# A convolution and spectral-mixing kernel: layout of the mixed modes, order of the band's set-up, of small copies and loads, and of the last stores

## The chip, the core and the metric

The kernel runs on one NeuronCore of a Trainium2 chip. The metric is the device time of one execution in microseconds (us), median of five runs. A core has five engines with a queue of instructions each: TensorE (PE in the profile; its weight loads are listed as PEld), VectorE (DVE), ScalarE (ACT), GpSimd (POOL) and SyncE (SP), and 16 DMA engines that move what SP, ACT and POOL issue. SBUF is the on-chip memory of 128 partitions; PSUM is where TensorE writes its results, eight banks of 512 float32 per partition.

## The reference

The input x is 8 x 3264 x 192 (batch, sequence, channels), float32. First a causal convolution over the sequence with 7 taps, whose softmaxed weights are one set for each of 8 heads of 24 channels. Then 64 Fourier modes of the result are mixed by complex 192 x 192 matrices, transformed back and added, and a dense layer with a ReLU comes on top.

```python
w = softmax(weight)                                   # 8 heads x 7 taps
a[b, s, h, :] = sum_k w[h, k] * x_padded[b, s + k, h, :]
X = rfft(a, axis=1)[:, :64]
Yr = Xr @ w_r - Xi @ w_i ; Yi = Xr @ w_i + Xi @ w_r   # one 192 x 192 pair for each mode
y = irfft(Y, n=3264, axis=1)                          # the other modes are zero
u = a + y
out = u + maximum(u @ w_ch, 0)
```

## The kernel before

Line numbers are those of the kernel before. The order of the instructions on each engine is the order of the Python text: there is no scheduler. The sequence is cut into 27 windows of 122 rows (`WIN`), each held with 6 more rows (`OV`) on 128 partitions, in one bfloat16 tile `x_all[partition, batch, window, channel]`. The last window has only 92 valid rows.

*Set-up.* SP loads eight windows of batch 0 as float32 (`x32`, L103), which ACT casts into `x_all` (L172); all the other windows come through POOL's DMA queue, which casts on the way (L61; the first window of batch 0 in two small pieces, L66 and L67). The taps come through ACT's queue (`wraw`, L99). DVE builds `diagc`, a band index of 38 columns for each group of 32 partitions (L146 to L149), and `ident` (L151), then the softmax of the taps (L166 to L179). TensorE spreads the taps over the partitions (L186). For each tap DVE makes a 128 x 304 product (`scaled`, L196: 8 heads x 38 columns) and TensorE adds it up through an identity into two PSUM banks, `bps`, both with the same content (L201). ACT copies the groups 0 and 2 of partitions out of one bank (L209), DVE the groups 1 and 3 out of the other (L211), into `cband`, the convolution's band matrix of each head.

*Convolution and DFT.* For each of 24 units (a batch and 8 to 10 windows) TensorE convolves (`conv_half`, L268), ACT or DVE writes the result back over the input (L275, L277), and TensorE adds the 64 modes over the windows (`dft_unit`, L290; the table `fst` is made by `f_turns` and `f_sin`). Only rows 0 to 121 of a window are written back. For windows 6, 13 and 20, rows 122 to 127 are therefore fetched from the next window by three SBUF-to-SBUF copies on SP (L366), since these windows are stored after their successors.

*Mixing.* The 64 modes are taken four at a time in 16 groups (`mix(g)`, L463), whose weights POOL loads ahead (`load_weights`, L259). Between the groups TensorE transposes the convolved rows into `cTa` and `cTb` (`t_next`, L426), and DVE and ACT copy them out. After each second group `mix_t` transposes the mixed values (L493) and DVE copies them into `yeT` (L494). `yeT` holds, for each of two halves of the channels, the mode components as outer index and the batch as inner one, so one batch is every eighth element. `y_back` transposes part of `yeT` back into `zy` (L485); the later groups reach `zy` by an SP DMA (L475). `prefill` starts the first output banks early, and `keep_warm` is a matmul without use.

*Output.* `zw_mm` multiplies `yeT` by the dense layer's matrix (L510). Then 108 units (half of the batches, window, pair of batches) follow: TensorE adds the dense layer of the convolved rows and the inverse transform (`z_ops`, L542), ACT applies the ReLU (L564), TensorE adds the inverse transform of the modes themselves (`y_ops`, L559), DVE adds the convolved rows (L594), and after each second unit SP stores 128 rows of four batches (L604), 384 KB; the window 26 goes out as 80 and 12 rows. The windows are taken in the order `worder`, by remainder modulo 7.

```python
    worder = sorted(range(NWIN), key=lambda w: (w % CH, w // CH))
```

Of the kernel before, what the change touches and what calls it, by code (L numbers as in the profile page):

```python
# [18 lines left out]
def kernel(  # L19
# [53 lines left out]
    def load_last():  # L73
# [29 lines left out]
    nc.sync.dma_start(out=x32[:], in_=bass.AP(tensor=x.tensor, offset=x.offset + (WIN * 10 - OV) * D,  # L103
                                              ap=[[D, P], [WIN * D, 8], [1, D]]))
# [4 lines left out]
    load_win(0, 1, 9)  # L109
    sidx = sp.tile([P, NWIN], F32, tag="sidx")  # L110
# [7 lines left out]
    load_unit(1, 0)  # L118
# [7 lines left out]
    for b in range(1, B):  # L126
        for u in range(3):
            if (b, u) != (1, 0):
                load_unit(b, u)
# [13 lines left out]

    NB = 32 + OV
    diagc = sp.tile([P, NB], F32, tag="diagc")
    nc.vector.memset(diagc[0:32, 0:OV], -1.0)  # L146
    for g in range(4):
        i0 = OV if g == 0 else 0
        nc.vector.tensor_copy(out=diagc[32 * g:32 * g + 32, i0:NB],  # L149
                              in_=diag[32 * g:32 * g + 32, 32 * g - OV + i0:32 * g + 32])  # L150
    nc.vector.tensor_scalar(out=ident[:], in0=diag[:], scalar1=0.0, scalar2=None, op0=ALU.is_equal)  # L151
# [29 lines left out]

    ps1 = ExitStack()
# [12 lines left out]
    for k in range(KK):  # L195
# [4 lines left out]
        for o in bps:  # L200
            nc.tensor.matmul(o[:, 0:H * NB], ident[:], scaled[:, k, :, :].rearrange("p h i -> p (h i)"),  # L201
                             start=(k == 0), stop=(k == KK - 1))
    make_k(1)
    for g in range(4):
        i0 = OV if g == 0 else 0
        dst = cband[32 * g:32 * g + 32, :, 32 * g - OV + i0:32 * g + 32]
        srcv = bps[g % 2][32 * g:32 * g + 32, 0:H * NB].rearrange("p (h i) -> p h i", h=H)[:, :, i0:NB]
        if g % 2 == 0:
            nc.scalar.copy(out=dst, in_=srcv)  # L209
        else:  # L210
            nc.vector.tensor_copy(out=dst, in_=srcv)  # L211
# [32 lines left out]
    yeT = constp.tile([P, 2, 2 * MODES * B], BF16, tag="yeT")  # L244
# [118 lines left out]


    for w in (6, 13, 20):
        nc.sync.dma_start(out=x_all[WIN:P, :, w, :], in_=x_all[0:OV, :, w + 1, :])  # L366
# [112 lines left out]
    def y_back(half):  # L479
        tp = pt.tile([P, 1024], BF16, tag="p", name="yb")  # L480
        n = 16 * YPE
        for i in range(4):
            for e in range(2):
                c0 = D * i + 64 * e
                nc.tensor.transpose(tp[0:n, c0:c0 + P], yeT[:, e, 4 * half + i:n * B:B], ident[:])  # L485
# [3 lines left out]
    def mix_t(g, ymix):  # L489
# [4 lines left out]
        nc.vector.tensor_copy(out=yeT[:, :, P * (g // 2):P * (g // 2) + P], in_=et)  # L494
# [261 lines left out]
```

## Time and profile before

| | |
|---|---|
| median of 5 runs | 180.55 us (180.28 to 181.05) |
| the profiled execution, its own time | 180.28 us |
| its span, first to last instruction | 178.5 us |
| PE busy, PEld busy | 149.3 us (84%), 130.4 us (73%) |
| DVE, ACT, POOL busy | 127.9, 112.6, 48.8 us |
| granted TensorE clock, mean | 0.994 |
| HBM read, written | 40.28 MB, 21.01 MB |
| last weights used from | 107.11 us |
| last DVE add ends | 173.79 us |

A span runs from an execution's first to its last instruction; the time of a run is some 1.8 us more. In the views, "us busy" of an engine is the sum of its instructions' times in a stretch, the DMA share is the mean busy share of the 16 DMA engines (packets that overlap count twice, so it can exceed 1), and GB/s is what they wrote: x and the weights arrive as float32 and are written as bfloat16, so a rate of 206 GB/s there is 412 GB/s read. The chain of waits goes back from the last instruction to whatever released each step.

### The profile page before, as it was taken

What the parts mean: (1) busy time and instruction counts of PE and PEld (TensorE: products, weight loads), DVE (VectorE), ACT (ScalarE), POOL (GpSimd) and SP (SyncE); (2) the same over time, 40 slices, a digit from 0 to 9 for tenths busy, and PEclk for the clock granted to TensorE, in tenths of its full rate; (3) what the DMA queues carried; (4) which work ended last, traced back from release to release, by engine and by line L of the source; (5) the groups of instructions that cost most, each with busy time, mean ns of one, the idle gap of its engine ahead of it and who ended that gap; (6) DMA issues with size and microseconds to landing.
All of it is one profiled execution on the core that took longest, in us unless ns stands there. A gap on an engine that the chain in (4) does not pass through costs nothing.

```text
span 178.5 us, 5425 instructions
## 1 busy us (share of the span) xinstructions
PE 149.3 (84%) x2132; PEld 130.4 (73%) x2132; DVE 127.9 (72%) x260; ACT 112.6 (63%) x188; POOL 48.8 (27%) x74
## 2 busy tenths in 40 slices
PE   0474779988899978887886978999999999999980
PEld 0243459878788868886775866799999999999950
DVE  5879975562553546966766425699999999999990
ACT  2356983555557635775766214588888888888850
POOL 7998342549222343541543000000000000000000
PEclk9999999999999999999999999999999999999997
DMA  4999999999999999999999980668999999999996
GB/s 132 212 190 192 192 192 192 191 190 192 192 192 195 202 206 208 204 207 207 205 208 205 208 145 11 208 222 281 373 357 327 368 339 355 346 311 368 339 327 229
DMA packets 65813, 42.04 MB, mean 236 GB/s; under 512 B 29212, under 2 KB 65788, under 8 KB 65788
## 3 DMA queue, kind: packets, MB, share of 16 engines
q0 software_dynamic: 36048, 19.75, 79.5%
q1 hardware_dynamic: 29738, 21.96, 37.1%
q8 instruction: 16, 0.26, 0.6%
q14 instruction: 9, 0.07, 0.1%
q10 hardware_dynamic: 2, 0.00, 0.0%
HBM read 40.28 MB, written 21.01 MB: 343 GB/s over the span
## 4 chain that ended last, share of the span: by engine, by line
PE 59%; DMA 17%; DVE 15%; issue 4%; POOL 1%; ACT 1%; DVEq 0%; POOLq 0%; ACTq 0%
PE z L542 19%; PE z L559 14%; DMA wt<-in_moe_w_i_dram 11%; PE xp L290 8%; PE cp L268 8%; DMA wt<-in_moe_w_r_dram 6%; DVE x_all L277 5%; PE tp L426 2%; PE bps L201 2%; PE yp L463 2%; PE tp L302 1%; DVE kprod L223 1%; PE z L524 1%; DVE xs L294 1%; DVE turns L221 1%
## 5 line engine op out<-in xcount | busy, mean ns | idle before, releaser
L594 DVE TENSOR_TENSOR t<-z,x_all 128x384 f32<-128x384 f32 x108 | 59.5, 557 | 3.3 <-PE z L559 1.7
L564 ACT ACTIVATE z<-z 128x384 f32<-128x384 f32 x108 | 50.9, 475 | 12.0 <-PE z L542 1.4
L542 PE MATMUL z<-zw,gst 64*128 64x384 bf16 x204 | 46.5, 323 | 0.0
L559 PE MATMUL z<-zy,gst 64*128 64x384 bf16 x204 | 46.2, 323 | 0.2
L542 PE MATMUL z<-win,cTa 64*128 64x192 bf16 x375 | 41.1, 243 | 0.0
L275 ACT CAST x_all<-cp 122x864 bf16<-122x864 f32 (+2 forms) x34 | 28.6, 879 | 16.5 <-PE cp L268 16.3
L542 PEld LDWEIGHTS <-cTa 64*128 64x128 bf16 x450 | 35.2, 94 | 2.7
L268 PE MATMUL cp<-x_all,cband 128*128 128x192 bf16 (+2 forms) x192 | 26.7, 293 | 7.5 <-DVE x_all L277 3.4
L268 PEld LDWEIGHTS <-cband 128*128 128x128 bf16 x192 | 20.1, 111 | 11.6 <-issue 4.2
L277 DVE CAST x_all<-cp 122x768 bf16<-122x768 f32 (+2 forms) x14 | 14.7, 1054 | 14.3 <-PE cp L268 13.9
L61 POOL DMA_DIRECT2D x_all<-in_x_dram x23 | 22.1, 974 | 8.1 <-DMA x_all<-in_x_dram 7.3
L290 PE MATMUL xp<-x_all,fst 122*128 122x192 bf16 (+1 forms) x216 | 22.3, 253 | 0.9 <-DVE x_all L277 0.5
L431 ACT COPY cTa<-tp 128x854 bf16<-128x854 bf16 (+1 forms) x16 | 14.0, 911 | 10.2 <-PE tp L426 10.1
L290 PEld LDWEIGHTS <-fst 122*128 122x128 bf16 (+1 forms) x216 | 18.6, 101 | 2.1 <-DVE x_all L277 0.7
L542 PEld LDWEIGHTS <-gst 64*128 64x128 bf16 x204 | 19.1, 94 | 0.6 <-issue 0.6
L542 PE MATMUL z<-win,cTb 64*128 64x192 bf16 x135 | 19.2, 243 | 0.0
L542 PE MATMUL z<-wB,cTa 64*128 64x192 bf16 x75 | 18.2, 243 | 0.0
L559 PEld LDWEIGHTS <-gst 64*128 64x128 bf16 x204 | 16.2, 93 | 1.0 <-POOLq L576 0.9
L542 PEld LDWEIGHTS <-cTb 64*128 64x128 bf16 x162 | 14.4, 94 | 1.1
L430 DVE COPY cTa<-tp 128x854 bf16<-128x854 bf16 (+1 forms) x17 | 10.6, 622 | 5.4 <-PE tp L426 5.0
L259 POOL DMA_DIRECT2D wt<-in_moe_w_r_dram x14 | 8.6, 612 | 19.9 <-PE tp L426 6.4
L426 PE MATMUL tp<-ident,x_all 122*128 122x122 bf16 x216 | 13.6, 217 | 0.0
(105 smaller groups left out, 172.0 us busy)
## 6 DMA issues: line engine op xcount, KB each, us to landing
out_dram<-t SPq DMA_DIRECT2D x52, 384.0 KB, 4.1
wt<-in_moe_w_r_dram POOLq DMA_DIRECT2D x14, 288.0 KB, 11.0
wt<-in_moe_w_i_dram POOLq DMA_DIRECT2D x14, 288.0 KB, 11.2
x_all<-in_x_dram POOLq DMA_DIRECT2D x8, 432.0 KB, 12.2
x_all<-in_x_dram POOLq DMA_DIRECT2D x7, 480.0 KB, 11.9
x_all<-in_x_dram POOLq DMA_DIRECT2D x8, 384.0 KB, 13.9
x<-in_x_dram SPq DMA_DIRECT2D x1, 768.0 KB, 5.0
fst<-in_moe_w_r_dram POOLq DMA_DIRECT2D x2, 288.0 KB, 10.3
```

Source lines behind the costliest of these rows:

```text
L61: nc.gpsimd.dma_start(out=x_all[:, b, c0:c0 + n, :], in_=src)
L268: nc.tensor.matmul(cp[:, j, 0:GRP * n].rearrange("p (w e) -> p w e", w=n), cband[:, h, :], x_all[:, b, w0:w0 + n, GRP * h:GRP * h + GRP], ...
L275: nc.scalar.copy(out=dst, in_=srcv)
L277: nc.vector.tensor_copy(out=dst, in_=srcv)
L290: nc.tensor.matmul(xp[:, 0:D], fst[0:k, c, :], x_all[0:k, b, c, :], start=(u == FIRST[b] and c == w0), stop=(u == LAST[b] and c == w0 + n ...
L426: nc.tensor.transpose(tp[:, WIN * k:WIN * k + WIN], slot_lhsT(p, k0 + k), ident[0:WIN, 0:WIN])
L430: nc.vector.tensor_copy(out=got[0][0], in_=got[0][1])
L431: nc.scalar.copy(out=got[1][0], in_=got[1][1])
L542: return nc.tensor.matmul(o, lhsT, rhs, start=start, stop=stop, skip_group_check=True, tile_position=(lo, 0))
L559: return [lambda: nc.tensor.matmul(zp[:, 0:2 * D], gst[lo:hi, WIN * w:WIN * w + P], zwi[(h, 1, k)][lo:hi, :], start=False, stop=(r == 1), ...
L564: return nc.scalar.activation(out=zp[:, 0:2 * D], in_=zp[:, 0:2 * D], func=ACT.Relu)
L594: add = nc.vector.tensor_tensor(out=t[:, 2 * k:2 * k + 2, :], in0=zp[:, 0:2 * D].rearrange("p (i e) -> p i e", i=2), in1=x_all[:, 4 * h + ...
```

## The change

Six things change, and nothing of what is computed. (1) The float32 load of eight windows becomes two loads of four, on SP and on ACT. (2) `diagc` and `ident` are made behind the softmax, and each `bps` bank holds four heads instead of all eight; ACT copies out the bank of the first four heads for all four groups of partitions, DVE the other. (3) The loads of batch 1's first two units are moved, the first ahead of the two small pieces of batch 0's first window. (4) `yeT` has the batch outside and the mode components inside, so one batch is contiguous; the copy of L494 now reads every eighth element. (5) Window 26 comes last in `worder`, and the three copies of L366 stand after the loop over the groups. (6) `y_back` stands after `mix_t`, and five matmuls without use follow in each of the groups 11, 12 and 13, into the bank (`junk`) that the third `prefill` takes later.

```diff
--- before.py
+++ after.py
@@ -100,13 +100,16 @@
                         in_=bass.AP(tensor=weight.tensor, offset=weight.offset, ap=[[H * KK, 1], [1, H * KK]]))
 
     x32 = sp.tile([P, 8, D], F32, tag="x32")
-    nc.sync.dma_start(out=x32[:], in_=bass.AP(tensor=x.tensor, offset=x.offset + (WIN * 10 - OV) * D,
-                                              ap=[[D, P], [WIN * D, 8], [1, D]]))
+    for q, eng in enumerate((nc.sync, nc.scalar)):
+        eng.dma_start(out=x32[:, 4 * q:4 * q + 4, :],
+                      in_=bass.AP(tensor=x.tensor, offset=x.offset + (WIN * (10 + 4 * q) - OV) * D,
+                                  ap=[[D, P], [WIN * D, 4], [1, D]]))
     load_unit(0, 2)
     diag = sp.tile([P, P], F32, tag="diag")
     nc.gpsimd.iota(diag[:], pattern=[[-1, P]], base=0, channel_multiplier=1,
                    allow_small_or_imprecise_dtypes=True)
     load_win(0, 1, 9)
+    load_unit(1, 0)
     sidx = sp.tile([P, NWIN], F32, tag="sidx")
     nc.gpsimd.iota(sidx[:], pattern=[[WIN, NWIN]], base=0, channel_multiplier=1,
                    allow_small_or_imprecise_dtypes=True)
@@ -115,7 +118,7 @@
     nc.gpsimd.iota(midx[:], pattern=[[1, MODES // 2], [MODES // 2, 2]], base=0, channel_multiplier=0,
                    allow_small_or_imprecise_dtypes=True)
     load_unit(0, 0)
-    load_unit(1, 0)
+    load_unit(1, 1)
     diag2 = sp.tile([P, MODES], F32, tag="diag2")
     nc.gpsimd.iota(diag2[:], pattern=[[-2, 2], [-4, MODES // 2]], base=0, channel_multiplier=1,
                    allow_small_or_imprecise_dtypes=True)
@@ -125,7 +128,7 @@
     wB0 = constp.tile([P, D], BF16, tag="wB0")
     for b in range(1, B):
         for u in range(3):
-            if (b, u) != (1, 0):
+            if (b, u) not in ((1, 0), (1, 1)):
                 load_unit(b, u)
         if b == 3:
             nc.gpsimd.memset(xt[:, :, 1, :, :], 0.0)
@@ -140,15 +143,6 @@
     ones = sp.tile([1, P], BF16, tag="ones")
     nc.vector.memset(ones[:], 1.0)
     nc.vector.memset(cband[:], 0.0)
-
-    NB = 32 + OV
-    diagc = sp.tile([P, NB], F32, tag="diagc")
-    nc.vector.memset(diagc[0:32, 0:OV], -1.0)
-    for g in range(4):
-        i0 = OV if g == 0 else 0
-        nc.vector.tensor_copy(out=diagc[32 * g:32 * g + 32, i0:NB],
-                              in_=diag[32 * g:32 * g + 32, 32 * g - OV + i0:32 * g + 32])
-    nc.vector.tensor_scalar(out=ident[:], in0=diag[:], scalar1=0.0, scalar2=None, op0=ALU.is_equal)
 
     halfpi = sp.tile([P, 1], F32, tag="halfpi")
     nc.vector.memset(halfpi[:], math.pi / 2)
@@ -179,6 +173,15 @@
     nc.vector.tensor_tensor(out=wrow[:], in0=wexp[:],
                             in1=wrec[:, :].unsqueeze(2).to_broadcast([1, H, KK]), op=ALU.mult)
 
+
+    NB = 32 + OV
+    diagc = sp.tile([P, NB], F32, tag="diagc")
+    nc.vector.memset(diagc[0:32, 0:OV], -1.0)
+    for g in range(4):
+        i0 = OV if g == 0 else 0
+        nc.vector.tensor_copy(out=diagc[32 * g:32 * g + 32, i0:NB],
+                              in_=diag[32 * g:32 * g + 32, 32 * g - OV + i0:32 * g + 32])
+    nc.vector.tensor_scalar(out=ident[:], in0=diag[:], scalar1=0.0, scalar2=None, op0=ALU.is_equal)
     ps1 = ExitStack()
     pconv = ps1.enter_context(tc.tile_pool(name="pconv", bufs=3, space=PSUM))
     pxx = ps1.enter_context(tc.tile_pool(name="pxx", bufs=1, space=PSUM))
@@ -197,18 +200,20 @@
                                        in0=diagc[:, :].unsqueeze(1).to_broadcast([P, H, NB]), scalar=float(k),
                                        in1=wsb[:, :, k:k + 1].to_broadcast([P, H, NB]),
                                        op0=ALU.is_equal, op1=ALU.mult)
-        for o in bps:
-            nc.tensor.matmul(o[:, 0:H * NB], ident[:], scaled[:, k, :, :].rearrange("p h i -> p (h i)"),
+        for half, o in enumerate(bps):
+            nc.tensor.matmul(o[:, 0:H // 2 * NB], ident[:],
+                             scaled[:, k, 4 * half:4 * half + 4, :].rearrange("p h i -> p (h i)"),
                              start=(k == 0), stop=(k == KK - 1))
     make_k(1)
     for g in range(4):
         i0 = OV if g == 0 else 0
-        dst = cband[32 * g:32 * g + 32, :, 32 * g - OV + i0:32 * g + 32]
-        srcv = bps[g % 2][32 * g:32 * g + 32, 0:H * NB].rearrange("p (h i) -> p h i", h=H)[:, :, i0:NB]
-        if g % 2 == 0:
-            nc.scalar.copy(out=dst, in_=srcv)
-        else:
-            nc.vector.tensor_copy(out=dst, in_=srcv)
+        for half, o in enumerate(bps):
+            dst = cband[32 * g:32 * g + 32, 4 * half:4 * half + 4, 32 * g - OV + i0:32 * g + 32]
+            srcv = o[32 * g:32 * g + 32, 0:H // 2 * NB].rearrange("p (h i) -> p h i", h=H // 2)[:, :, i0:NB]
+            if half == 0:
+                nc.scalar.copy(out=dst, in_=srcv)
+            else:
+                nc.vector.tensor_copy(out=dst, in_=srcv)
 
 
     WFAC = -TWOPI * (1.0 - 4e-7) / S
@@ -241,7 +246,7 @@
 
     gst = constp.tile([P, GW], BF16, tag="gst")
 
-    yeT = constp.tile([P, 2, 2 * MODES * B], BF16, tag="yeT")
+    yeT = constp.tile([P, 2, B, 2 * MODES], BF16, tag="yeT")
 
 
 
@@ -360,10 +365,6 @@
 
     ps1.close()
     conv_stack.close()
-
-
-    for w in (6, 13, 20):
-        nc.sync.dma_start(out=x_all[WIN:P, :, w, :], in_=x_all[0:OV, :, w + 1, :])
     workp = early_stack.enter_context(tc.tile_pool(name="work", bufs=3, side="right"))
     tailp = early_stack.enter_context(tc.tile_pool(name="tails", bufs=2, side="right"))
     pza = ctx.enter_context(tc.tile_pool(name="pza", bufs=3, space=PSUM))
@@ -482,7 +483,7 @@
         for i in range(4):
             for e in range(2):
                 c0 = D * i + 64 * e
-                nc.tensor.transpose(tp[0:n, c0:c0 + P], yeT[:, e, 4 * half + i:n * B:B], ident[:])
+                nc.tensor.transpose(tp[0:n, c0:c0 + P], yeT[:, e, 4 * half + i, 0:n], ident[:])
         nc.vector.tensor_copy(out=zy[0:n, 4 * half:4 * half + 4, :],
                               in_=tp[0:n, 0:4 * D].rearrange("p (b e) -> p b e", b=4))
 
@@ -491,7 +492,9 @@
         et = zt[:, 256:512].bitcast(BF16)[:, 0:2 * P].rearrange("p (t k) -> p t k", t=2)
         for t in range(2):
             nc.tensor.transpose(et[:, t, :], ymix[:, 64 * t:64 * t + P], ident[:])
-        nc.vector.tensor_copy(out=yeT[:, :, P * (g // 2):P * (g // 2) + P], in_=et)
+        q = 16 * (g // 2)
+        nc.vector.tensor_copy(out=yeT[:, :, :, q:q + 16],
+                              in_=et.rearrange("p t (q b) -> p t b q", b=B))
 
 
 
@@ -507,7 +510,7 @@
             zp = banks[i % len(banks)]
             o = zp[:, D * i:D * i + D] if len(banks) == 1 else zp[:, 0:D]
             for e, wn in ((0, win0), (1, win1)):
-                nc.tensor.matmul(o, yeT[:, e, b:2 * MODES * B:B], wn[:, :],
+                nc.tensor.matmul(o, yeT[:, e, b, :], wn[:, :],
                                  start=(e == 0), stop=(e == 1), skip_group_check=True)
         zt = zwip.tile([P, 2 * D], BF16, tag=f"zw{h}{k}", name="zw")
         if len(banks) == 2:
@@ -605,7 +608,7 @@
 
 
     CH = 7
-    worder = sorted(range(NWIN), key=lambda w: (w % CH, w // CH))
+    worder = sorted(range(NWIN), key=lambda w: (w == NWIN - 1, w % CH, w // CH))
     wq = [(0, worder[0]), (0, worder[1])]
     for i in range(2, NWIN):
         wq.append((0, worder[i]))
@@ -626,13 +629,13 @@
         return py.tile([P, 512], F32, tag="y", name="z")
 
     def prefill():
-        zps.append(bank(len(zps)))
+        zps.append(junk if len(zps) == 2 else bank(len(zps)))
         ab_full(seq[len(zps) - 1], zps[-1])
 
-    def keep_warm(n):
+    def keep_warm(o, n):
 
         for _ in range(n):
-            nc.tensor.matmul(zwps[0][:, 0:P], ident[:], ident[:], start=True, stop=True)
+            nc.tensor.matmul(o[:, 0:P], ident[:], ident[:], start=True, stop=True)
 
     for g in range(NGRP):
         last = g == NGRP - 1
@@ -656,19 +659,27 @@
 
             if g in (10, 11, 14):
                 prefill()
-            if g in (12, 13):
-                y_back(g - 12)
+            if g == 11:
+                junk = bank(2)
         else:
-            keep_warm(4)
+            keep_warm(zwps[0], 4)
         if m is not None:
             mix_t(g, m)
+        if g in (12, 13):
+            y_back(g - 12)
+        if g in (11, 12, 13):
+            keep_warm(junk, 5)
         if g == NGRP - 2:
             zwps += [pt.tile([P, 512], F32, tag="p", name="zwps") for _ in range(2)]
             prefill()
             prefill()
-            keep_warm(6)
+            keep_warm(zwps[0], 6)
+
+
+    for w in (6, 13, 20):
+        nc.sync.dma_start(out=x_all[WIN:P, :, w, :], in_=x_all[0:OV, :, w + 1, :])
     zwps.append(py.tile([P, 512], F32, tag="y", name="zwps"))
-    keep_warm(4)
+    keep_warm(zwps[0], 4)
     early_stack.close()
 
     padp = ctx.enter_context(tc.tile_pool(name="pad", bufs=1, side="right"))
```

## The prediction

> **What bounds the kernel now.** I read the chain of waits first, then windows of DMA load, then the rows of the lines that the diff touches. The execution has three stretches: loading (0 to 107 us), a hinge (107 to 113), and the output stretch (113 to 174) with a store drain behind it.
>
> Windows view (columns: stretch, its length, busy us and count of PE, PEld, DVE, ACT, POOL, granted clock, DMA share, GB/s):
>
> ```profile
> 20.00:22.00 2.00, 1.77 (x10) 1.38 (x11) 1.93 (x5) 2.00 (x4) 0.98 (x1) 1.00 1.60 191
> 62.00:64.00 2.00, 2.00 (x26) 1.92 (x27) 0.62 (x2) 1.39 (x3) 0.91 (x2) 1.00 1.21 207
> 64.00:66.00 2.00, 1.51 (x17) 1.12 (x15) 1.06 (x1) 0.55 (x1) 0.92 (x2) 1.00 1.20 205
> 66.00:68.00 2.00, 1.05 (x23) 0.74 (x23) 1.01 (x6) 0.00 (x0) 0.61 (x1) 1.00 1.21 206
> 104.00:104.50 0.50, 0.05 (x1) 0.13 (x1) 0.50 (x2) 0.00 (x0) 0.00 (x0) 1.00 1.22 207
> 105.50:106.00 0.50, 0.50 (x9) 0.50 (x7) 0.00 (x0) 0.00 (x0) 0.00 (x0) 1.00 0.71 134
> 106.00:106.50 0.50, 0.50 (x11) 0.50 (x8) 0.00 (x0) 0.00 (x0) 0.00 (x0) 1.00 0.14 28
> 106.50:107.00 0.50, 0.19 (x4) 0.01 (x1) 0.00 (x0) 0.00 (x0) 0.00 (x0) 1.00 0.03 5
> ```
>
> From 5 us on the DMA moves a flat 190 to 194 GB/s while x comes in and 205 to 208 while weights come in, at a share over 1. Nothing that PE, DVE or ACT do makes a dent in it. So loading ends when the bytes are through, and a faster head cannot end it earlier. The last three lines show something else: the 16 engines do not end together. A share of 0.14 is some two engines, 0.03 less than one. The load rate falls from 105 us, yet the last weights land only at 107.1.
>
> The chain of waits (start, length, what) shows that landing and what follows it:
>
> ```profile
> 96.86 10.21 DMA wt<-in_moe_w_i_dram
> ...
> 107.11 0.51 PE yp L463 x12
> ...
> 108.47 0.30 DVE yeT L494
> ...
> 108.82 0.57 PE zwps L510 x4
> ...
> 111.72 0.33 PE zwps L510 x4
> ```
>
> Behind the hinge PE is full: 10.00 us busy of each 10, one unit of 384 columns every 0.57 us (chain steps 115.72, 116.29, 116.86), at clock 1.00. Then the stores drain:
>
> ```profile
> 171.00:172.00 1.00, 1.00 (x16) 0.70 (x12) 0.98 (x3) 0.90 (x3) 0.00 (x0) 1.00 0.94 280
> 172.00:172.50 0.50, 0.50 (x6) 0.10 (x2) 0.50 (x2) 0.40 (x2) 0.00 (x0) 1.00 0.68 208
> 172.50:176.50 4.00, 0.75 (x4) 0.18 (x2) 1.75 (x4) 0.12 (x1) 0.00 (x0) 0.97 1.09 370
> 176.75:177.00 0.25, 0.00 (x0) 0.00 (x0) 0.00 (x0) 0.00 (x0) 0.00 (x0) 0.50 0.32 108
> ```
>
> 370 GB/s is the ceiling of stores. A store of 393 KB every two units (1.145 us) is 343 GB/s, so stores fill 93% of it, and the last four (172.5 to 176.5) run back to back.
>
> **The change part by part.**
>
> *Band by halves, softmax ahead of diagc.* L201 runs 14 matmuls of 304 columns in 3.72 us; 14 of 152 at half the spacing take 1.9, so the seven DVE products (2.79 us from 6.66) set the pace and the sums are ready about 1.1 us earlier. Eviction becomes four copies per engine: ACT 2 x 0.38 becomes 4 x about 0.29, DVE 2 x 0.47 becomes 4 x 0.32, +0.3 us each (estimates by the fixed part of those rows). The softmax moves before diagc (1.6 us) and fills the wait for the iota; 0 to 0.4 us sooner if the weights have landed by 2.5 us, 0.4 later if only by 3. Head: 0.4 to 1.2 us earlier. Cover: the x transfers. [...] Worth 0.
>
> *x32 on two queues.* The single load lands 5.0 us after its issue, and 3.25 to 4.75 us already runs at 362 to 381 GB/s, all the engines carry. [...] The table load on ACT slips by some 0.4 us into a wait of 2.4 us. Between -0.2 and +0.2 (the ACT half caught behind POOL's loads) I take 0, the row's side.
>
> *Small x loads later.* Two POOL issues (0.61 and 0.54 us) fall behind one of 1.02; the index iotas move with them, to about 5.4 us, and kprod needs those at 9.4. Their data, on today's landing, comes some 2.5 us later (one 480 KB load at 192 GB/s), by 13 us; the unit that reads it starts at 17. The queue holds several us of work. 0.
>
> *Spilled-row copies behind the weights.* Three SP issues (0.72 to 0.95 us) leave 61.7 to 65.9 and come after the second zy store, whose issue ends at 108.66. They end by about 111.1; the next on SP is the first store at 112.22, so 1.1 us of cover. If it is gone, a late store costs nothing until eight output buffers are full, about 9 us. Readers of the rows come tens of us later. What they free is DMA time under the weights: 55 KB at 207 GB/s is 0.27 us, with the dip of 2 and 1 GB/s in the windows 0.3. They have six rows each, so perhaps six engines carry it all: 0.8 us on those. If the engine that ends last is one of them, loading ends up to 0.8 sooner; if not, 0. I take -0.25, near the even spread.
>
> *Contiguous yeT.* Rows of the touched lines (ns min/median/max):
>
> ```profile
> L510 PEld LDWEIGHTS <-yeT x16: 142/144/171, 108.8 to 111.7; 128*128 128x128 bf16 x16
> L532 PEld LDWEIGHTS <-cTa x24: 95/98/100, 94.2 to 112.2; 128*128 128x128 bf16 x24
> L494 DVE COPY yeT<-yp x8: 277/292/292, 72.7 to 108.5; 128x256 bf16<-128x256 bf16 x8
> ```
>
> The copy now reads PSUM with a step of eight. [...] Once, for the last group, this is on the path; seven times it hides under weights. Against it stands a faster weight load. [...] The loads partly overlap the matmuls (0.33 us for four in the chain either way), so I count one exposed load in each of three groups, 3 x 0.046 = -0.14. Net 0, between -0.2 and +0.2. The y_back transposes (L485, loads of 273 ns) get shorter, before 104 us, under the weights.
>
> *y_back after mix_t, 15 warming matmuls, junk bank.* The clock is 1.00 there already. 15 x about 0.06 us in a stretch where PE waits for weights (1.18 us at 98.4, 0.42 at 107.1), and mix_t no longer stands behind y_back's 1.57 us. 0; without that cover +0.3 at most.
>
> *Shortest block last.* The last store falls from 393 to 283 KB, sent as 80 and 12 rows. At 370 GB/s that is -0.30 us if the queue is empty when it starts. But today's two short blocks give a dip just before the last four stores (280 and 208 GB/s), in which lagging engines catch up; then the bytes only change places and it is worth 0. The second issue (0.37 us later) caps the gain too. -0.1, between -0.35 and +0.3.
>
> **Sum.** -0.25 + 0 - 0.1 = -0.35 on the profiled execution's span of 178.5, so 178.15. That execution took 180.28, 1.78 around the span, so 179.93; the median of the runs, 180.55, stands 0.27 above it: 180.2.
>
> **Rivals.**
>
> *The last engine was a carrier of the copies, and the queue drains empty.* -0.7, -0.3 and -0.1: about 179.4. For it: the lone engines after 106 us. Against it: the rate at 64 to 68 us hardly dips.
>
> *The head counts.* The chain of waits does run through bps, cband and turns. If the saved 0.4 to 1.2 us reached the end, with the sum above, about 179.4 too. Against it: the flat DMA rate.
>
> *Slower: an instruction fetch meets the wrong engine.* The page's DMA part has
>
> ```profile
> q8 instruction: 16, 0.26, 0.6%
> ```
>
> 0.6% of 16 engines x 178.5 us over 16 packets is 1.07 us of one engine for each 16 KB block. PE's list grows by 15 matmuls and 15 loads ahead of the last weights, so blocks fall due at other moments. A block on the engine already last, in the last 10 us of the weights, holds the landing of 107.1 back by up to 1.07, nothing else waiting; from 0.9 on it outweighs the gains by over 0.3%. With the sum: 180.55 - 0.35 + 1.07, about 181.3. For it: one engine's straggle decides this landing already. Against it: there are some eight blocks in 107 us for 16 engines.
>
> *The change does not do what it says.* The strided copy's price eats the loads, the copies were free, the tail conserves work: 180.5.
>
> **How the numbers follow.** A measurement of this kernel can tell about 0.3%, 0.54 us, from no change: the bounds are 180.0 and 181.1. Forecast case (180.2, own range 179.8 to 180.6) 0.50, of which a third is below 180.0; the two fast rivals together 0.20; nothing changes 0.20; fetch 0.10. Faster 0.36, same 0.55, slower 0.09. Leaving out about 2 in 10: 179.3 to 181.0.
>
> **What would show it.** Right: weights landing at 106.6 to 107.1, three x_all copies after 108.7 us, LDWEIGHTS of L513 near 98 ns, the yeT copy near 0.42, first conv matmul about 11 instead of 12 us with no effect at 107, last issue to end 0 to 0.3 us shorter. Wrong: loading ends before 106.3 or after 107.6, a yeT copy over 0.6, PE idle between 113 and 170, or first stores waiting behind the copies.

## The result, and the profile after

The changed kernel takes 181.53 us (median of 30 runs, 180.13 to 183.51); the kernel before, run beside it, 180.53. The ratio is 1.0043 with a 95% interval of 1.0028 to 1.0057: slower by 0.4%, where 180.2, in a range of 179.3 to 181.0, had been forecast. Ratios and intervals leave out the executions that took over 1.5% longer than the fastest one of their kernel.

The profiled execution is such a long one: 183.22 us, more than all but one of the 30, span 181.5. It is read for where a long execution loses its time, and beside it stands the profile of a second measurement of the same kernel (e1 below; 181.0 us, the sixth shortest of 19, span 179.1). No profile caught an execution of this kernel at its median. Line numbers from here on are those of the kernel that a line is taken from, mostly the changed one. Times below that no view prints are taken from the trace's own records. Three stretches make up each execution up to its last stored byte:

| us | before | after | after again (e1) |
|---|---|---|---|
| first matmul of the last group: the last weights have landed | 107.11 | 107.95 | 106.45 |
| from there to the end of the last DVE add | 67.15 | 68.39 | 67.23 |
| from there to the last byte stored | 2.93 | 3.80 | 4.13 |
| last byte stored | 177.19 | 180.14 | 177.82 |

(The last add of before ends at 174.26 us by its trace, 107.11 + 67.15, and not at 173.79 as its table has it.) So the loss is not in one place. The landing is later in one execution and earlier in the other, the middle is either 0.08 or 1.24 us longer, and the drain is longer in both.

Windows of the changed kernel at the end of the loading (columns as in the prediction; the last two are DMA share and GB/s):

```profile
105.50:106.00 0.50, 0.50 (x7) 0.50 (x8) 0.00 (x0) 0.00 (x0) 0.00 (x0) 1.00 0.44 82
106.00:106.50 0.50, 0.50 (x10) 0.50 (x8) 0.00 (x0) 0.00 (x0) 0.00 (x0) 1.00 0.20 36
106.50:107.00 0.50, 0.42 (x8) 0.25 (x5) 0.00 (x0) 0.00 (x0) 0.00 (x0) 1.00 0.15 25
107.00:107.50 0.50, 0.00 (x0) 0.00 (x0) 0.00 (x0) 0.00 (x0) 0.00 (x0) 1.00 0.12 22
```

The rate falls off sooner than before (82 GB/s where it was 134), and then a share of 0.12 to 0.20 goes on for 1.5 us: two or three of the 16 engines carry what is left, and PE has nothing to do. The chain of waits goes through that landing, and shows the second loss right behind it:

```profile
97.85 10.06 DMA wt<-in_moe_w_i_dram
...
107.95 0.51 PE yp L464 x11
...
109.32 0.43 DVE yeT L496
...
109.80 0.99 PE zwps L513 x8
110.78 0.40 PE z L527
111.18 0.64 PE zwps L513 x4
111.82 1.92 PE z L527 x6
```

Eight L513 matmuls took 0.99 us and six L527 matmuls 1.92, 0.32 each, where 384 columns go through in 0.16 at a clock of 1.00 (an L527 matmul at 114.14 us in the same chain). The windows show the clock (the third number from the end), first in the changed kernel, then in the one before over the same part of the hinge:

```profile
109.00:110.50 1.50, 1.14 (x14) 0.87 (x14) 0.75 (x2) 0.16 (x1) 0.00 (x0) 0.95 0.13 33
110.50:113.50 3.00, 3.00 (x13) 1.68 (x12) 1.74 (x5) 1.85 (x5) 0.00 (x0) 0.50 0.12 26
```

```profile
109.50:113.00 3.50, 3.35 (x27) 2.22 (x26) 3.12 (x7) 2.37 (x7) 0.00 (x0) 1.00 0.05 11
```

From 110.34 to 113.75 us the granted clock is 0.50, and PE gets through 13 matmuls in three microseconds. From there on the output stretch has the pace of before, so the 1.2 us are never won back. The profile of e1 has no such fall.

The page's DMA part has one more instruction block than before (17 packets for 16):

```profile
q8 instruction: 17, 0.28, 0.6%
```

The rows of the touched lines came out as the prediction had them (the landing, for which it had 106.6 to 107.1, did not):

```profile
L496 DVE COPY yeT<-yp x8: 413/424/426, 71.7 to 109.3; 128x256 bf16<-128x256 bf16 x8
L513 PEld LDWEIGHTS <-yeT x16: 95/101/147, 109.8 to 113.8; 128*128 128x128 bf16 x16
L680 SPq DMA_DIRECT2D x_all<-x_all x3: 727/751/893, 109.7 to 111.7; - x3
L486 PEld LDWEIGHTS <-yeT x16: 121/123/127, 100.4 to 103.7; 128*96 128x96 bf16 x16
```

The copy costs 0.42 us instead of 0.29, the loads 101 ns instead of 144, and those of y_back 123 instead of 273. The three copies of the spilled rows now run behind the last weights.

### The profile page after: what moved, and what is told of

Same layout as the page of the kernel before. It is cut to its first block, busy times and chain, and to the rows that moved or that the text cites. A ratio compares the mean times of both kernels' runs of the same rounds, so it can differ in the third digit from the quotient of the medians.

```text
span 181.5 us, 5457 instructions
## 1 busy us (share of the span) xinstructions
PE 148.3 (82%) x2147; PEld 128.8 (71%) x2147; DVE 130.1 (72%) x262; ACT 113.7 (63%) x190; POOL 49.0 (27%) x74
## 4 chain that ended last, share of the span: by engine, by line
DMA 53%; DVE 31%; PE 6%; POOL 3%; issue 2%; DVEq 0%; ACT 0%; POOLq 0%; ACTq 0%
DVE t L597 31%; DMA x_all<-in_x_dram 30%; DMA wt<-in_moe_w_i_dram 23%; POOL x_all L61 3%; PE z L527 2%; PE z L545 1%; PE zwps L513 1%; PE yp L464 1%; POOL wt L264 1%; PE tp L427 1%; DVEq L762 0%; DVE yeT L496 0%; ACT ymix L473 0%; PE z L562 0%; PE z L535 0%
## 5 line engine op out<-in xcount | busy, mean ns | idle before, releaser
L464 PEld LDWEIGHTS <-xt 128*32 128x32 bf16 x192 | 5.2, 146 | 12.3 <-issue 6.6
L464 PE MATMUL yp<-wt,xt 128*32 128x192 bf16 x168 | 6.7, 263 | 8.7 <-DMA wt<-in_moe_w_i_dram 4.2
```

The source lines that it names most:

```text
L464: nc.tensor.matmul(zt[32 * pos:32 * pos + 32, 0:D], xt[:, j, half:half + 2, :, MG * i + pos].rearrange("p s k -> p (s k)"), wtiles[g][:, p ...
```

## The experiments

Each kernel was timed against the kernel before on the same chip; the medians of before were 180.5 to 180.7. A ratio is to that kernel, with its 95% interval. "Before plus" means that one part of the change was put into the kernel before, "after minus" that it was taken out of the changed one.

### First round: the clock, the engines, or the layout

Three theories are meant by letters in what was expected: C, the clock falls in the hinge; D, some DMA engines lag and the last weights land late; E (from the second round on), the order of the last stores costs time.

**e1**, the changed kernel again, no edit.

> The changed kernel again, on the chip on which the next three are timed. Theory C (clock): in the profile of the changed kernel the granted clock falls to 0.50 between 110.5 and 113.5 us, the hinge takes 7.5 us from the landing of the last weights instead of 6.3, so +1.2 us. Theory D (DMA): two engines lag, the last weights land 0.85 us later, whatever PE does. Both expect 181.0 to 182.0 here (ratio 1.003 to 1.008); C expects a clock of 0.5 in the hinge again, D a landing after 107.6 again.

181.47 us, ratio 1.0037 (1.0011 to 1.0064). The slowdown is there again.

**e2**, after plus 21 useless matmuls around the last groups.

```diff
-            keep_warm(junk, 5)
+            keep_warm(junk, 12 if g == 13 else 5)
-            keep_warm(zwps[0], 6)
+            keep_warm(zwps[0], 14)
-            keep_warm(zwps[0], 4)        # in two places
+            keep_warm(zwps[0], 7)
```

> The changed kernel with 7 + 8 + 3 + 3 more matmuls without use in the gaps of PE around the last two mixings, nothing else. Theory C: the clock stays at 1.00 through the hinge and about 1.2 us come back where it fell, median 180.3 or so. Theory D: nothing comes back, 181.0 to 182.0, since the weights land as late as before.

181.51, ratio 1.0034 (1.0014 to 1.0054): more work for PE does not bring the time back, so the clock is not what sets the median. (The profile of e2 is of its shortest execution, 180.13 us, where the weights land at 106.54 us and the clock holds.)

**e3**, after minus the contiguous yeT; **e4**, before plus the contiguous yeT.

```diff
-    yeT = constp.tile([P, 2, 2 * MODES * B], BF16, tag="yeT")
+    yeT = constp.tile([P, 2, B, 2 * MODES], BF16, tag="yeT")     # e4; e3 the reverse
...  (the copy into yeT and the reads of it follow)
```

> The changed kernel with the old layout of yeT (a batch is every eighth element again), all else as changed. Theory C: the y_back transposes take 1.57 us each again instead of 0.61, so PE is fuller before the hinge, and the clock stays up: 180.2 to 180.6. Theory D: 181.0 to 182.0.

> The kernel before with the contiguous yeT alone. Theory C: it suffices to drop the clock in the hinge in some executions, 181.0 or more, since y_back loses 1.9 us of PE work and no warming matmul is added. Theory D: 180.4 to 180.7, like the kernel before; the yeT copy 0.42 and the LDWEIGHTS of zw_mm 98 ns in either case.

e3: 180.8, ratio 1.0009 (0.9985 to 1.0032). e4: 181.08, ratio 1.0015 (0.9993 to 1.0036); nine of its runs lie between 180.3 and 180.6, thirteen between 181.1 and 182.0. In both profiles of these kernels the middle stretch is as short as before, to 0.09 us. Neither interval is clear of 1, and that of e3, which lies between its two expectations, overlaps that of e1. So the layout may take part in the loss; its own instructions do not.

### Second round: one part at a time

**e5**, before plus window 26 last; **e8**, after minus it.

```diff
-    worder = sorted(range(NWIN), key=lambda w: (w % CH, w // CH))
+    worder = sorted(range(NWIN), key=lambda w: (w == NWIN - 1, w % CH, w // CH))
```

> The kernel before with one part of the change: window 26 is the last of the output order, so the last issue of a store is the short one (80 and 12 rows). Three theories of what the change adds. C (the clock falls for one window of 3.4 us in the hinge, because of the new PE work there) and D (lagging DMA engines, because of the moved loads, copies and instruction fetches) have nothing to act on here: the same as before, 180.5 to 180.7, with the last data 2.9 to 3.0 us behind the last DVE add as before. E (the tail): in the profiles with window 26 last the last data came 3.3, 3.8 and 4.1 us behind the last DVE add where it was 2.9 with the old order (3.2 in two other runs with the old order), so this alone costs 0.3 to 0.9 us: 180.9 to 181.5. The prediction's own step says -0.1, between -0.35 and +0.3: 180.4.

> The changed kernel with the old output order (window 26 fourth from the end). E: the drain (last DVE add to last data) goes back from 3.3 to 4.1 us to 2.9 to 3.2, and the time from 181.5 to 180.7 to 181.1. C and D, and the contiguous yeT as the only cause (undoing it gave 180.8): stays at 181.4 to 181.5.

e5: 180.7, ratio 0.9995 (0.9981 to 1.0009), drain 2.94 us. e8: 182.32 (six runs), ratio 1.0084 (1.0053 to 1.0114), drain 3.86. Theory E falls: the order of the windows costs nothing, and the drain stays long without it. e8 came out above everything that had been expected of it; why its six executions are 0.85 us longer than those of e1 is open.

**e6**, before plus the three copies behind the weights.

```diff
-    for w in (6, 13, 20):
-        nc.sync.dma_start(out=x_all[WIN:P, :, w, :], in_=x_all[0:OV, :, w + 1, :])
     workp = early_stack.enter_context(...)
...
+    for w in (6, 13, 20):
+        nc.sync.dma_start(out=x_all[WIN:P, :, w, :], in_=x_all[0:OV, :, w + 1, :])
     zwps.append(py.tile([P, 512], F32, tag="y", name="zwps"))
```

> The kernel before with one part of the change: the three copies of the spilled rows stand behind the loop over the groups. The prediction's step: weights landed 0 to 0.8 us sooner, -0.25: 180.3. D: the landing is set by which engine lags and that is drawn anew with every execution, so a median gain of at most 0.1 and a landing between 106.4 and 108 in the profile. A copy that blocks SP's first store would show as a later first store (after 113.5) but not in the end. C and E: the same as before.

180.25, ratio 0.9975 (0.9963 to 0.9987); landing 106.66 instead of 107.11. This part is a gain of 0.45 us.

**e7**, before plus the two-queue load of x32 and the new order of POOL's loads.

> The kernel before with one part of the change: float32 load of eight windows as two loads on two queues, and batch 1's first two units moved in POOL's order. The prediction's step: 0, 180.5 to 180.6. D: another order of the loads shifts which engines lag when the weights end, so the landing moves by up to +-0.7 us: 180.0 to 181.2, and a larger spread. C and E: the same as before.

180.9, ratio 1.0007 (0.9986 to 1.0029), with four of 22 runs above 181.7. So in the kernel before the moved loads cost 0.2 us or so, not clear of nothing; the fourth round comes back to that.

### Third round: the lagging engines

For each load or weight block the trace holds 16 landings (those of `x32` in before come from 5.52 to 5.79 us), read here as one for each DMA engine. They tell how far behind the first engine the last ones end, though not which engines these are. In the profile of after this lag is at most 0.35 us on a load that the first engine finished at 5.1 us; on the one finished at 7.2 three engines are 1.6, 1.9 and 2.1 us behind, and they are still so at 12.1. On the weights of 104.7 us the last three are 1.9, 2.8 and 3.2 us behind. In the profile of before all 16 are within 0.31 us at 12 us, and the last one is 2.1 us behind at 105.

**e10**, after minus the moved loads; **e11**, the same with e2's useless matmuls; **e12**, after minus moved loads and contiguous yeT; **e9**, before plus contiguous yeT and ten useless matmuls.

```diff
-    for q, eng in enumerate((nc.sync, nc.scalar)):       # e10, e11, e12
+    nc.sync.dma_start(out=x32[:], ...)                   # and the old order of load_unit
...
-            keep_warm(6)                                 # e9
+            keep_warm(16)
```

> The changed kernel with the old x32 load and the old order of the x loads. Theory D: the moved loads leave one or two DMA engines 2.3 to 3.2 us behind the first instead of 1.6 to 2.0, so that the last weights land up to 1.4 us later in some runs; undone, the landing goes back to about 106.6, the runs above 182 disappear, and the median is 180.6 to 181.0 with the clock's second mode still there. Theory C alone: no change, 181.3 to 181.5.

> The changed kernel with the old loads and 21 more matmuls without use around the last groups of the mixing (as in the run with more warming). C and D together: neither the late landing nor the fall of the clock is left, so the gain of the moved copies shows: 180.2 to 180.5. D alone: the same as with the loads undone. C alone (loads innocent): 181.4 to 181.5, as the warming alone had.

> The changed kernel with the old yeT and the old loads; what is left of the change is the band by halves, y_back behind mix_t with 15 warming matmuls, the copies behind the weights and window 26 last. C and D: the gain of the copies alone, 180.1 to 180.4. If band, y_back's place or the last window cost something that is not seen yet: 180.6 to 181.

> The kernel before with the contiguous yeT alone and ten more matmuls without use (keep_warm(6) becomes 16) just ahead of the last group of the mixing. Theory C in its present form: the clock is set for each stretch of 3.41 us of a grid that is not tied to the kernel; in the ten profiles so far every stretch after which the clock fell while the kernel was busy (20 to 165 us) had matmuls worth under 0.40 of a full array (columns x active rows x active columns), and with the old yeT no stretch over the landing of the last weights is under 0.41. The contiguous yeT makes y_back shorter (0.3 to 0.6 us in place of 1.57), so PE's fill ends 1.0 instead of 0.6 us ahead of the landing, and the stretch falls to 0.32 to 0.37; when the clock falls there, the 384-column matmuls behind it take 0.50 instead of 0.32 us, +1.2 us. C: ten matmuls of 128 columns (0.055 us each) close 0.55 us of that gap, the stretch rises to about 0.5, the second mode that the contiguous yeT alone showed (13 of 22 runs between 181.1 and 182.0) goes, and the median comes to 180.6 to 180.8 (before plus 0.09). Rival: the contiguous yeT costs by itself (copy, loads, order): the runs stay bimodal, median 181.0 to 181.2.

e10: 180.5, ratio 0.9991 (0.9965 to 1.0017). e11: 180.44, 0.9985 (0.9969 to 1.0001). e12: 180.37, 0.9978 (0.9961 to 0.9994). In the changed kernel the moved loads carry about 1 us, the whole of the loss. With them away, the layout of yeT is worth 0.1 us (e10 against e12), and 21 more warming matmuls bring nothing (e11). The loads undone gave slightly more than theory D had expected. e9 was a miss for both theories: 181.34, ratio 1.0036 (1.0019 to 1.0053), in one group, with the clock at 1.00 in the hinge and the landing at 106.98. Its loss is in the drain: 4.02 us. Its trace has an instruction block of 16 KB at 172.7 us, in the middle of the last stores; so have after, e1, e2, e3, e8 and e10 to e12 (1.5 to 4.2 us before the last add), and before and e4 to e7 have none there. (The page lists these packets as instruction, q8. That they belong to PE's instructions is the author's reading of a count: of all 20 profiles the twelve with more matmuls than before have a block there, the eight others none.)

### Fourth round: which load, and the instruction block

**e13**, after minus the x32 split alone; **e14**, after minus the new order of POOL's loads alone.

> The changed kernel with x32 as one load on SP again; the new order of POOL's loads stays. If the split over two queues makes the engines lag (the slow packets, 70 to 560 ns in place of 51, come at 5 to 7 us, just where ACT's half ends and POOL's loads begin): no slow packets, the third-last engine under 0.45 us behind at 12 us, landing 106.4 to 106.7, 180.4 to 180.7 us. If the order does it: as the changed kernel, 181.3 to 181.6.

> The changed kernel with the old order of POOL's loads; x32 stays on two queues. The mirror of the run before it: 181.3 to 181.6 with slow packets at 5 to 7 us if the split does it, 180.4 to 180.7 if the order does. Both near 180.9: each does a half, or only both together.

e13: 180.53, ratio 0.9993 (0.9974 to 1.0011). e14: 181.64, ratio 1.0044 (1.0027 to 1.0061). Of the moved loads it is the split that does it: 20 of e14's 22 runs are above 181, three of e13's 14. The windows where ACT's half of x32 ends and POOL's loads begin, first after, then e13:

```profile
5.00:5.50 0.50, 0.00 (x0) 0.00 (x0) 0.49 (x2) 0.00 (x0) 0.50 (x2) 1.00 1.43 169
5.50:6.00 0.50, 0.00 (x0) 0.10 (x1) 0.45 (x4) 0.45 (x1) 0.50 (x2) 1.00 1.42 169
6.00:6.50 0.50, 0.06 (x1) 0.06 (x1) 0.50 (x2) 0.50 (x1) 0.50 (x2) 1.00 1.46 161
6.50:7.00 0.50, 0.50 (x4) 0.34 (x4) 0.50 (x2) 0.50 (x1) 0.50 (x1) 1.00 1.38 153
```

```profile
5.00:5.50 0.50, 0.00 (x0) 0.00 (x0) 0.49 (x2) 0.00 (x0) 0.50 (x2) 1.00 1.56 191
5.50:6.00 0.50, 0.00 (x0) 0.10 (x1) 0.45 (x4) 0.28 (x1) 0.50 (x2) 1.00 1.57 189
6.00:6.50 0.50, 0.06 (x1) 0.06 (x1) 0.50 (x2) 0.50 (x1) 0.50 (x2) 1.00 1.60 193
6.50:7.00 0.50, 0.50 (x4) 0.34 (x4) 0.50 (x2) 0.50 (x1) 0.50 (x1) 1.00 1.60 193
```

PE, DVE and POOL do the same on both sides, ACT nearly; the last two columns differ. (191 + 189 + 193 + 193 - 169 - 169 - 161 - 153) GB/s x 0.5 us = 57 KB less in two microseconds, 0.3 us of all engines or 1.6 us of three. In after eleven packets of POOL's queue took 75 to 527 ns there instead of 51. Two microseconds of a stretch that is over 100 us from the end look harmless on average; but the three lags are all there 95 us later, with more on top: at a DMA share of 1.6 (12 to 60 us in after) and then 1.21 (60 to 104 us) they were not made up. This is the end of the loading in e13:

```profile
105.50:106.00 0.50, 0.06 (x2) 0.00 (x0) 0.00 (x0) 0.00 (x0) 0.00 (x0) 1.00 0.51 96
106.00:106.50 0.50, 0.04 (x4) 0.04 (x6) 0.00 (x0) 0.00 (x0) 0.00 (x0) 1.00 0.03 6
106.50:107.00 0.50, 0.50 (x15) 0.38 (x16) 0.00 (x0) 0.00 (x0) 0.00 (x0) 1.00 0.00 0
```

Done by 106.1 us instead of 107.6, and the last group starts at 106.46. In e14's profile the landing is 107.40, and the clock falls as in after:

```profile
109.50:113.00 3.50, 3.50 (x19) 2.28 (x17) 2.06 (x5) 2.00 (x5) 0.00 (x0) 0.52 0.16 36
```

The split costs that much only together with something else in the change, since in the kernel before it cost 0.2 (e7). What that is no run settles, but the 20 profiles point to the band's new order. The largest lag at 12 us is over 1 us in seven of them, and all seven have the new order: five of its six with the split (after, e1, e3, e8, e14; not e2) and two of its six without (e11 with 2.4, e16 with 1.7 us, both long executions). With the old order it is at most 0.8 us, in e7. The new order brings the softmax and the band's products forward: between 5 and 7 us DVE is busy for 1.94 or 1.95 us in all twelve profiles that have it, and for 1.2 to 1.3 in the other eight. By itself the new order costs nothing (e18 below). Part of the split's cost may also be hidden in the kernel before, whose last engine is 2.1 us behind at 105 us anyway, with the three copies still among the weights. A run with the split and the old order in the changed kernel would tell.

**e15**, before plus ten useless matmuls and nothing else; **e16**, after minus contiguous yeT, moved loads and the 15 useless matmuls.

```diff
-            keep_warm(6)           # e15
+            keep_warm(16)
-        if g in (11, 12, 13):      # e16
-            keep_warm(junk, 5)
```

> The kernel before with ten more matmuls without use ahead of the last group (keep_warm(6) becomes 16), nothing else. Fetch theory: 20 more instructions of PE carry its list over the edge of one more 16 KB block, whose fetch falls at about 1.5 us before the last DVE add; the drain becomes 3.5 to 4.1 us instead of 2.9, and the time 181.1 to 181.4, as with the contiguous yeT and the same ten matmuls (181.34). Rival: the loss there was the yeT's: 180.6 to 180.7 here, whatever the fetch.

> The changed kernel with the old yeT, the old loads and without the 15 useless matmuls: band by halves, y_back behind mix_t, copies behind the weights and window 26 last are left. Fetch theory: no fetch in the last 6 us of the stores, drain 2.9 to 3.2 us, 179.9 to 180.2, faster than with the 15 matmuls (180.37) and than the copies alone (180.25). Rival (the fetch is harmless three microseconds ahead of the end): 180.3 to 180.4.

e15: 181.26, ratio 1.0031 (1.0011 to 1.0051). e16: 179.93, ratio 0.9968 (0.9947 to 0.9989), and 0.44 us below e12, from which only the 15 matmuls are gone; the two intervals overlap. The DMA view of 170 to 180 us (packets, MB, share), first e15, then e16:

```profile
q1 hardware_dynamic: 3284, 2.43, 72.5%
q8 instruction: 1, 0.02, 0.7%
```

```profile
q1 hardware_dynamic: 3323, 2.45, 74.7%
```

In e15 the block sits on one engine from 172.35 us for 1.11 us. In the last store of e15 fifteen engines are done by 177.67 us and one at 178.37; in before the last two end at 177.48 and 177.52. The end of the drain in windows of before and of e15:

```profile
176.00:177.00 1.00, 0.00 (x0) 0.00 (x0) 0.00 (x0) 0.00 (x0) 0.00 (x0) 0.64 0.85 289
177.00:178.00 1.00, 0.00 (x0) 0.00 (x0) 0.00 (x0) 0.00 (x0) 0.00 (x0) 0.50 0.02 8
```

```profile
176.00:177.00 1.00, 0.00 (x0) 0.00 (x0) 0.00 (x0) 0.00 (x0) 0.00 (x0) 1.00 0.81 274
177.00:178.00 1.00, 0.00 (x0) 0.00 (x0) 0.00 (x0) 0.00 (x0) 0.00 (x0) 0.75 0.10 35
```

A share of 0.10 is one or two engines. The last byte comes 3.84 us after the last add instead of 2.93, while landing and middle are as before (107.05 and 67.15 us). With the ten matmuls, 20 instructions with their loads, e15's page counts 17 such blocks like after's, where e16's counts 16 like before's. Single drains scatter, though: 3.10 to 4.14 us in the twelve profiles with such a block, 2.69 to 3.50 in the eight without. The 3.50 is e7's, and unexplained.

### Last round: the version that beats both

**e17**, e16 plus the contiguous yeT; **e18**, e16 with the old band and softmax order.

> The version with only the helpful parts (179.93 against a kernel before of 180.66) plus the contiguous yeT. Clock theory: two modes, one 0.1 us above that version (180.0) and one 1.2 us higher (181.2), since y_back is short again and no useless matmul fills the gap before the last weights; median 180.2 to 181. Copy theory (only the copy's 0.09 us counts): 180.0, one mode. By the prediction's own step (0): 179.9.

> The same version with the old band and softmax order; left are the copies behind the weights, window 26 last and y_back behind mix_t. The prediction's step (band worth 0, hidden by the loading): 179.9. If the earlier head counts after all: 180.2, as the copies alone.

e17: 179.84, ratio 0.9958 (0.9936 to 0.9980), with four of 22 runs at 180.9 to 181.2, about as many as e16 and e18 have there; e10 is e17 with the 15 matmuls and takes 0.66 us more, a second pair for their cost. e18: 180.0, ratio 0.9973 (0.9952 to 0.9993). The contiguous yeT costs nothing here, and the band is worth at most 0.1 us, less than can be told. All of e16 to e18 beat both kernels; what they share beyond e6 is window 26 last and y_back behind mix_t. Against e6 (0.9975) they are not clearly faster.

### The clock in the hinge

The 20 profiles show a pattern for it, found after the fact. Between 25 and 165 us every fall lasts 3.41 us, and in each trace its falls lie on one grid of that step, whose place differs from trace to trace (in after the fall at 178.61 us, behind the last matmul, comes 68.27 us, 20 steps, after the one at 110.34). For every stretch of the grid from 25 to 165 us I summed columns x active rows x active columns of its matmuls, as a share of a full array at 384 columns in 0.16 us. Of some 800 stretches at full clock, eight were followed by a fall, and all eight lie at or under 0.391; four others under it had no fall; above it, from 0.394 on, none fell. In three profiles the stretch over the hinge was such a one: after (0.39), e8 (0.36) and e14 (0.34), and these are the three that have the contiguous yeT, no more than 15 useless matmuls and a landing past 107.3 (107.95, 107.43, 107.40). With the same layout and a landing up to 107.1 the clock held (e1, e4, e10, e13, e17), with the old layout even at 107.75 (e16), and with more useless matmuls at 108.75 (e11). With the contiguous layout PE runs out of work 0.85 to 1.0 us ahead of the last weights (ten or 21 useless matmuls more: 0.4 to 0.7), where it was 0.4 in before, e5 and e6.

That the late landing matters is not shown, however; where the grid happens to lie explains the three falls as well. Moved over the hinge in small steps, a stretch of 3.41 us is at or under 0.391 in 19% to 30% of its positions in each of the eight profiles with the contiguous layout and no more than 15 useless matmuls, early landing or late; in e16 and e18 (old layout, none of the 15) in 18% and 6%; in the other ten in none. By that estimate at most about one execution in four of the changed kernel would have the fall, which moves its median little. The three with a fall are among the longest of their runs (183.22, 182.70 and 182.73 us).

In after the window that was followed by the fall (106.9 to 110.3) had PE busy for 1.86 of its 3.41 us.

## Why the prediction was wrong

- **The step that failed most: "x32 on two queues", set to 0 between -0.2 and +0.2.** In the changed kernel it costs 1.0 us (after and e1 181.5, e14 181.6, e13 180.5). The step asked when the bytes of this load arrive, and the average rate over 100 us. The landing is set by the slowest engine (in after the last group's weights land from 104.67 us on, the last of the 16 at 107.91, and the group starts at 107.95), and in five of the seven profiles with the split one to three of them are 1.0 to 2.1 us behind by 12 us. Eight instruction blocks of 0.89 to 0.98 us fall into the loading of after, each one packet and so on one engine. The landing varies from run to run (106.45 in e1, where the last engine's lag only went from 1.3 to 1.6); that it does so by which engines the blocks meet is the author's reading, not shown. No run shows the -0.2 that the step had at its better end. Each part was also priced alone: the split in the kernel before (e7) shows 0.2, so what it costs depends on another part, which stays open.
- **Warming matmuls: "0; without that cover +0.3 at most".** Ten of them alone cost 0.6 us (e15, clear of noise), the 15 of the change 0.44 (e12 to e16) or 0.66 (e10 to e17), within the noise of each pair. It is not by their running time: in e15 the landing and the middle are as before, and the drain is 0.91 us longer (3.84 for 2.93), with one 16 KB block more, of 1.11 us, among the last stores. The rival of the prediction, an instruction fetch that meets the wrong engine, had named such a block and nearly the total (181.3), but put it on the weights' landing. There too a lag grew as a block came: in after the last landing of a load is 2.1 us behind the first up to 42.9 us, and 3.15 from 45.2 on, with a block of 0.98 us at 45.0. The rival was given 0.10 because it was thought of as a draw over 16 engines; at the drain a block falls in all twelve profiles with these matmuls. That the rival's total is close is in part luck, since most of the loss is the split's.
- **Contiguous yeT: net 0.** Right by itself in the median (e17 against e16: -0.1; the middle stretch is 67.23 or 67.24 us in all eight profiles that have it and no fall of the clock there, 67.15 or 67.16 without it). The net set a copy of 0.42 against -0.14 for the loads. No row of before shows what a read with a step of eight costs; the runs showed 424 ns instead of 292 for the copy's 256 elements, so 0.42 was met. (The rates that before does show, in its wider forms: 122 elements more cost a bf16 copy (L430) 65 ns, 96 more a cast (L277) 99.) Missed was that with the shorter y_back PE runs out of work earlier, 0.85 to 1.0 us ahead of the last weights instead of 0.4, and that in three of the profiles with this layout the clock falls in the hinge, where 1.1 to 1.2 us are lost. "The clock is 1.00 there already" was true of one profile. Undoing the layout in the changed kernel was worth 0.67 us (e1 to e3), not clear of noise; that the clock is the reason is not shown.
- **Copies behind the weights: -0.25.** Right in kind, undersized: -0.45 (e6).
- **Band: 0, new order of the small loads: 0, window 26 last: -0.1.** Each by itself right within what can be told: e18, e13 and e5. The head did start 1.8 us earlier (0.4 to 1.2 had been worked out), with no effect at 107 by itself. That the band's new order is the split's partner, and so not free, is possible and untested.
- **The sum.** 180.66 - 0.45 + 1.0 + 0.44 to 0.6 gives 181.65 to 181.8; measured were 181.5. The terms were measured in different kernels, so that they add up this closely is in part luck. The range ended at 181.0 because two bounds on unknown costs were drawn from averages.

Open: why POOL's packets are slow at 5 to 7 us (in five of seven profiles with the split, and also without it, most in e11 and e16), and the upper group of e4, of which there is no profile.

## What to carry to other kernels

With the DMA share at 1.2 to 1.6 from 12 to 104 us, the last engine's delay of 2.1 us at 7 us in after was not made up (3.2 at 105 us), so judge an edit to early loads by the last engine's lag, over several executions, and not by the rate. An edit whose cost alone can't be told from nothing can cost 1 us beside another: the moved loads did (0.2 in e7, 1.0 between after and e10). Useless matmuls were not free even where PE waits (ten cost 0.6 us in e15): count the instruction blocks on the page before and after, and look where the new one falls. Undo parts one by one even of a change that looks small, since here gains of 0.45 us and more were hidden by two costs.

## What was not expected of the hardware

- The clock fell for 3.41 us after eight of the twelve windows of that length whose matmuls filled 0.391 of the array or less, with PE busy 42% to 65% of the time in the eight; after none of the other windows, some 800.
- A 16 KB instruction block held one DMA engine for 0.88 to 2.0 us, 16 or 17 times in an execution of these kernels.
- Weight loads with a column step of eight took 144 ns for 128 columns and 273 ns for 96 (medians of 16 in before), contiguous ones 101 and 123 (in after).
